# Pairs of neighbouring PSUM banks for score runs, and new rule tables for the order planner of a gated attention + MLP kernel

## The chip, the core and the metric

The kernel runs on one core of one Trainium2 chip. The metric is the device time of one execution in microseconds (us); the time before is 664.01 us, the median of three runs (663.37 to 664.15). A core has a matmul engine (PE), which writes only into PSUM (8 banks of 128 partitions x 512 fp32 here), and three engines that work on tiles: ACT (exponentials), DVE and POOL. SP issues most of the transfers. Each engine takes its instructions strictly from its own list and stops at the first one whose semaphores are not yet up; so the order of each list is decided before the kernel runs.

## What is computed

Two branches over the same 2048 x 512 input are mixed by a gate. In the kernel, everything is bf16 with fp32 sums in PSUM.

```python
x = A_x
g = _sigmoid((x * gate_w).sum(-1, keepdims=True))
# a: 32 heads of 16: qkv = x @ wqkv; scores = q k^T / 4; p = softmax(scores); o = p v; a = o @ wo
# b: (x @ w_gate) * (x @ w_up) @ w_down, inner width 1376
return g * a + (1 - g) * b
```

The scores are 32 heads x 2048 x 2048, and each needs an exponential: this is what ACT, and in part DVE, spend their time on.

## The kernel before, in words

**Tiles on PE.** Almost every matmul uses a 64 x 32 part of the array. The 128 rows are split in two halves (`r` = 0 or 1 in the code), the 128 columns in four. A *batch* is four matmuls of 512 columns on one half, one for each column part (`pe64`; with new weights it shows as L1674, with weights that are still held from the batch before as L1652). Two batches on different halves stream at the same time. One pass of both halves, eight matmuls, is called a *turn* below.

**Three kinds of batches.** *Scores* (`QM,KT`): the keys of 128 positions against 512 queries, one bank for each head of a group of four heads; 2,048 banks in all. *PV* (`Vp` or `Vs` as weights): the exponentiated scores times V, with a column of ones for the denominators. *Fill* (`u`, `g`, `k`, `q`, `v`, `do` units; weights named `xT`, `wu`, `wg`, `wd`, `wk`, `wq`, `wo`): projections, the MLP and the output. A fill unit takes 8 batches in most cases and then a single evacuation of one bank; a score batch takes one evacuation for each batch.

**Two kinds of score steps.** A step is four heads x 128 keys x 512 queries. An *A* step is exponentiated by ACT (`exp`, L1771) from PSUM into cells of `PT` or of buffers that are free at the time (`xT`, `wd`, `wu`, `wg`, `wo`, `hT`); one instruction can take two banks if they are neighbours. It has two PV batches. A *D* step is done on DVE by writing integers whose bits are a bf16 exponential (`dpass`, L1811, into `DB`, `wv`, `wk`); three shifted copies of it are made by POOL (L1818) or DVE (L1817), and PV runs over the four versions with scaled V, eight batches, so that the error averages out. So a D step costs PE six batches more than an A step.

**The planner.** `_Sched` simulates the engines while it writes their lists. Whenever half `r` is free in its model, `pe_phase` (L677) offers it, in a fixed order, the start of an A score (`s_a`, L313), of a D score (`s_d`, L343), a PV batch (`v_job`, L388) or a fill batch (`f_cont`, `f_start`). Some 35 named rules (how many A scores may be outstanding, how far one half may run ahead, how long ACT waits for a neighbour, and so on) are tables over the model's time: `g(name)` (L177) reads the entry for the present slot of 4 us. `bank_pick` (L273) chooses one of the free banks; for A scores it looks for one next to the bank taken last, or one that has a free neighbour, but it takes one bank at a time, and nothing keeps the neighbour for the mate. `try_act` (L741) joins two ready A scores in one instruction where their banks are neighbours. The delays in this model (0.216 us for a batch, 0.05 us from an engine's end to the next engine's start, and so on) are constants in the code. `emit` then turns the dependencies into semaphore waits.

Of the kernel before, what the change touches and what calls it, by code (L numbers as in the profile page):

```python
# [136 lines left out]
class _Sched:  # L137
# [134 lines left out]

    def bank_pick(self, kind, r):  # L273

        fr = self.bfree
        if kind == "A":
# [24 lines left out]
        best = None  # L301
# [10 lines left out]

    def s_a(self, r):  # L313
# [11 lines left out]
        bank = self.bank_get("A")  # L325
# [8 lines left out]
        self.log("pe%d" % r, 0.216, ("SA", e.q, e.kt, ci, bank))  # L334
        self.take(r, 0.216)
# [7 lines left out]
    def s_d(self, r):  # L343
        i = self.dpos[r]
        if not self.bfree or self.nb["D"] >= self.g("dmax"):
            return False
        if len(self.bfree) <= self.g("ares") and self.nb["A"] < self.g("amin"):
            return False
        if i - self.dpos[1 - r] >= self.g("skewd") or (self.g("lw") > 1 and i % 2 == 0 and len(self.bfree) < 2):
            return False  # L350
# [6 lines left out]
        bank = self.bank_get("D", r)  # L357
# [8 lines left out]
        self.log("pe%d" % r, 0.216, ("SD", e.q, e.kt, ci, bank))  # L366
        self.take(r, 0.216)
# [20 lines left out]
    def v_job(self, r):  # L388
# [43 lines left out]
        self.ofree[p] = self.now + 0.385 + 0.05  # L432
        self.at(self.ofree[p])
        self.log("pe%d" % r, 0.216, ("V", e.q, e.kt, e.kind, v))
        self.take(r, 0.216)
        done = self.now + 0.385 + 0.05
# [124 lines left out]
    def f_slice(self, u, r):  # L561
# [15 lines left out]
        self.log("pe%d" % r, u.slot, ("F", u.name, r, i))  # L577
        self.take(r, u.slot)
        if u.pos == u.n:
            end = self.now + 0.385 + max(0.0, u.slot - 0.216)  # L580
            if u.ph == 0:
                u.ph, u.half, u.pos = 1, 1 - r, 0
                u.okt = end + 0.07
# [45 lines left out]
    def f_start(self, r):  # L629
# [4 lines left out]
        if sum(1 for u in self.fact if u.ph == 0) >= self.g("fstart"):  # L634
            return False
# [94 lines left out]

    def evenly(self, l):
# [9 lines left out]
    def try_act(self):  # L741
# [26 lines left out]
        if grp is not None:  # L768
# [3 lines left out]
            if len(fr) > 1:  # L772
                for i in range(len(rd)):
                    j = next((j for j in range(i + 1, len(rd)) if abs(rd[j][4] - rd[i][4]) == 1), None)
                    if j is not None and (i == 0 or self.g("apick")):
# [5 lines left out]
                        if self.g("tri"):  # L781
                            lo, hi = min(x[4], y[4]) - 1, max(x[4], y[4]) + 1
                            z = next((z for z in rd if z[4] == lo or z[4] == hi), None)
# [8 lines left out]
                if n == 1 and any(abs(x[4] - rd[0][4]) == 1 and x[0] <= self.now + self.g("await") for x in self.aready):  # L792
# [10 lines left out]
        dur = 0.42667 * n + 0.0635  # L803
# [10 lines left out]
        t = self.now + dur + 0.11 + 0.05  # L814
# [67 lines left out]
    def dve_pass(self, now):  # L882
        mate, hold = None, False
        if self.dready and self.dready[0][0] <= now and self.g("dpair"):
            x = self.dready[0]
            for y in sorted(self.dready, key=lambda y: y[:2])[1:]:
                if abs(y[4] - x[4]) == 1 and (y[2] is x[2] or max(x[2].buf, y[2].buf) < self.par["ND"]):
# [4 lines left out]
        if self.dready and self.dready[0][0] <= now and (mate or not hold):  # L892
# [17 lines left out]
            self.at(t + 0.05, lambda: [self.bank_put(b, [op]) for b in bks])  # L910
            for y in xs:
# [4 lines left out]
                if e.npass == 4:  # L916
# [5 lines left out]
                    for r in (0, 1):  # L922
                        self.vq[r].append((t + 0.05, e, 0, e.ydone))
                    self.at(t + 0.05)
# [10 lines left out]
    def copy_dve(self):  # L935
        now = self.now + 1e-9
        for e in self.cpq:
# [17 lines left out]
            self.cp_done(e, v, hs, op, self.now + dur + self.DEND + 0.05)  # L955
# [124 lines left out]
    def q_evac(self, c, b):  # L1080
        def f(sc, u, last):
# [3 lines left out]
            sc.at(sc.now + 0.681 + 0.05, lambda: sc.bank_put(bk, [op]))  # L1085
            sc.at(sc.now + 0.681 + 0.05, lambda: (sc.qpend.append((k, op)), sc.q_try()))
# [31 lines left out]
    def o_evac(self, m, vops):  # L1118
# [14 lines left out]
        t = self.now + 0.681 + 0.05  # L1133
# [90 lines left out]
    def norm3(self, bi, o):  # L1224
# [3 lines left out]
        self.setr(("ot", bi), self.now + 0.598 + self.DEND + 0.05, op)  # L1228


    def simple(self, dur, dend, key, make, after=None):


        def f(sc, u, last):
            op = make(u, last) if sc.hw else None
            bk = u.bank
            t = sc.now + dur + dend + 0.05
# [7 lines left out]
    def setup(self):  # L1245
# [29 lines left out]
        def mk_x(ch, t):  # L1275
            def ev(sc, u, last):
# [3 lines left out]
                tq = sc.now + ND + DE + 0.05  # L1280
# [69 lines left out]
        def mk_do(c, tt):  # L1350
            t = 4 * c + tt

            def ev(sc, u, last):
# [9 lines left out]
                tq = sc.now + 0.658 + DE + 0.05  # L1363
# [123 lines left out]
    def run(self):  # L1487
# [17 lines left out]
        self.aout = self.dout = 0  # L1505
        self.aready, self.dready = [], []
# [76 lines left out]
class _Hw:  # L1583
# [179 lines left out]
    def exp(self, banks, cells, deps):  # L1763
        g, i = cells[0]
        t = self.grp[g]
        if len(banks) > 1:
            dst = t[:, i : cells[-1][1] + 1 : cells[1][1] - i, :]
            src = self.ps[:, banks[0] : banks[-1] + 1, :]
# [227 lines left out]
    def prologue(self):  # L1996
# [113 lines left out]
        for var in (0, 1):  # L2110
# [22 lines left out]
 'alook': ((127, 2), (1, 3), (9, 2), (2, 6), (41, 2)),  # L2133
# [3 lines left out]
 'amax': ((1, 4), (2, 3), (1, 6), (2, 5), (1, 4), (2, 5), (21, 4), (6, 5), (24, 4), (2, 5), (6, 7), (1, 6), (20, 4), (1, 7), (1, 4), (1, 6), (1, 5),  # L2137
          (30, 4), (2, 7), (3, 4), (1, 5), (1, 4), (2, 5), (5, 4), (2, 6), (2, 4), (3, 6), (1, 4), (1, 6), (5, 4), (3, 6), (6, 5), (20, 6)),
 'amin': ((7, 4), (5, 3), (8, 1), (16, 3), (2, 1), (11, 0), (1, 1), (2, 3), (4, 0), (1, 3), (3, 0), (2, 2), (6, 3), (1, 1), (5, 2), (5, 0), (2, 1),
          (4, 3), (6, 0), (1, 3), (2, 2), (4, 3), (1, 2), (1, 0), (1, 2), (1, 3), (2, 2), (4, 4), (5, 2), (6, 1), (1, 0), (9, 3), (3, 0), (19, 3),  # L2140
          (8, 2), (1, 3), (20, 2)),
 'apick': ((12, 1), (1, 0), (23, 1), (33, 0), (5, 1), (5, 0), (4, 1), (8, 0), (2, 1), (1, 0), (4, 1), (1, 0), (20, 1), (9, 0), (1, 1), (11, 0),
           (1, 1), (2, 0), (3, 1), (5, 0), (2, 1), (7, 0), (20, 1)),
 'ares': ((3, 2), (9, 1), (1, 3), (1, 2), (6, 1), (1, 3), (4, 2), (7, 3), (4, 2), (10, 3), (4, 0), (1, 2), (5, 1), (4, 2), (2, 1), (6, 0), (1, 1),
          (1, 2), (4, 1), (1, 0), (1, 2), (3, 3), (1, 1), (3, 2), (7, 1), (1, 2), (1, 3), (2, 2), (4, 0), (14, 2), (3, 3), (4, 2), (1, 1), (4, 3),
          (1, 1), (3, 3), (1, 0), (3, 2), (9, 3), (3, 2), (2, 3), (5, 2), (5, 0), (3, 2), (1, 3), (20, 2)),
 'await': ((1, 0.6), (2, 0), (3, 0.2), (1, 0.3), (3, 0.1), (4, 0), (3, 0.1), (19, 0), (17, 0.05), (2, 0), (5, 0.05), (2, 0), (6, 0.05), (1, 0),
           (3, 0.05), (2, 0.1), (5, 0.05), (1, 0.1), (5, 0.05), (2, 0), (4, 0.05), (1, 0.3), (6, 0), (8, 0.1), (2, 0.4), (3, 0.05), (1, 0.1),
           (13, 0.05), (4, 0), (1, 0.1), (2, 0), (9, 0.05), (10, 0), (9, 0.05), (20, 0)),
 'cpmax': ((1, 20), (2, 14), (3, 8), (1, 14), (1, 20), (2, 8), (2, 10), (24, 14), (12, 10), (1, 3), (1, 30), (10, 14), (2, 30), (7, 14), (5, 5),  # L2150
           (5, 10), (1, 20), (1, 10), (2, 8), (2, 10), (2, 8), (4, 30), (6, 5), (1, 20), (2, 5), (1, 10), (11, 5), (3, 8), (2, 20), (2, 30), (1, 8),
           (5, 30), (7, 8), (3, 30), (6, 8), (5, 30), (1, 20), (1, 10), (3, 20), (7, 14), (2, 3), (20, 14)),
 'dact': ((10, 2), (2, 5), (2, 2), (10, 5), (1, 3), (2, 2), (7, 3), (15, 2), (1, 4), (7, 2), (3, 3), (9, 5), (2, 2), (3, 4), (11, 2), (6, 5), (19, 2),
          (7, 5), (15, 2), (3, 4), (2, 5), (2, 3), (2, 5), (6, 2), (1, 5), (6, 2), (26, 3)),
 'dahead': ((3, 0), (3, 1), (2, 2), (2, 0), (1, 2), (1, 0), (1, 1), (11, 2), (1, 1), (4, 2), (7, 0), (5, 2), (2, 1), (10, 2), (7, 1), (8, 2), (1, 1),
            (10, 2), (1, 1), (1, 2), (2, 1), (32, 2), (2, 1), (9, 2), (2, 1), (7, 2), (6, 1), (5, 2), (2, 1), (3, 0), (9, 2), (20, 0)),
 'dend': ((1, 2), (1, 0), (1, 5), (3, 2), (2, 0), (4, 2), (5, 1), (3, 4), (8, 1), (2, 3), (7, 1), (5, 3), (10, 2), (4, 5), (9, 2), (1, 5), (17, 0),
          (4, 2), (3, 0), (1, 2), (6, 3), (1, 2), (2, 3), (1, 5), (1, 3), (8, 0), (5, 3), (7, 0), (3, 2), (7, 1), (3, 2), (2, 1), (4, 3), (2, 0),
          (1, 1), (2, 0), (1, 2), (1, 4), (3, 3), (29, 4)),
# [146 lines left out]
```

## Time and profile before

| | |
|---|---|
| median of three runs | 664.01 us |
| the profiled execution, first to last instruction (its span) | 667.2 us |
| PE | 658.8 us busy, 22,835 matmuls |
| ACT | 647.0 us busy, 995 instructions |
| DVE | 605.0 us busy, 1000 instructions |
| POOL | 548.8 us busy, 640 instructions |
| granted TensorE clock | 0.999 |

The profiled execution's own time is its span, 3.2 us above the median. A busy PE in this table is a PE with at least one matmul in flight: with two halves, one of them may stand still while the engine counts as busy. So the number of matmuls in a stretch of time says more than the busy share. The busy times of ACT and DVE include the end of an instruction that overlaps the next one's start, so that durations in the groups are longer than the distance from start to start.

### The profile page before, as it was taken

To read this page: it belongs to the slowest core of one execution; us is meant where nothing else is said; L and a number is where in the kernel's file an instruction comes from. 1 tells how busy PE (TensorE), PEld (TensorE's weight loads), DVE (VectorE), ACT (ScalarE), POOL (GpSimd) and SP (SyncE) were. 2 spreads that over 40 slices of the span, in tenths; PEclk is the share of its full clock that TensorE was granted. 3 is DMA by queue.
4 is the path that set the end of the run, shared out by engine and by line. 5 is a ranking of instruction groups with operands and counts; after the bars stand their busy time and mean duration, and the time that the engine had idled before them with its cause. 6 is when DMAs were issued, how large, how long until landed. Compare 5 with 4: busy or idle time off the path is not lost.

```text
span 667.2 us, 47435 instructions
## 1 busy us (share of the span) xinstructions
PE 658.8 (99%) x22835; PEld 368.4 (55%) x20907; DVE 605.0 (91%) x1000; ACT 647.0 (97%) x995; POOL 548.8 (82%) x640
## 2 busy tenths in 40 slices
PE   8999999999999999999999999999999999999997
PEld 4565555565555555555555565555555565555553
DVE  6899989999998998999999898999999887898885
ACT  5999999999999999999999999999999999999995
POOL 3576899898999868998998879899998997784781
PEclk9999999999999999999999999999999999999999
DMA  9201211212221100001011010100001010000101
GB/s 177 61 5 30 65 31 50 61 28 55 74 61 26 38 20 26 26 12 30 13 21 29 16 42 21 31 13 17 25 14 28 21 38 23 16 25 15 34 21 36
DMA packets 32120, 22.95 MB, mean 34 GB/s; under 512 B 17356, under 2 KB 28524, under 8 KB 31920
## 3 DMA queue, kind: packets, MB, share of 16 engines
q1 hardware_dynamic: 30784, 18.86, 11.5%
q8 instruction: 171, 2.80, 1.8%
q0 software_dynamic: 176, 0.53, 0.3%
q10 hardware_dynamic: 960, 0.52, 0.3%
q14 instruction: 29, 0.24, 0.1%
HBM read 12.23 MB, written 2.36 MB: 22 GB/s over the span
## 4 chain that ended last, share of the span: by engine, by line
PE 98%; DMA 1%; DVE 1%; issue 0%; ACT 0%; ACTq 0%
PE ps L1674 88%; PE ps L1652 9%; DMA wq<-in_A_wqkv_dram 1%; PE ps L2086 0%; DVE hT L1956 0%; DVE hT L1953 0%; ACT wu L1771 0%; ACTq L2003 0%; DVE wu L1860 0%; PE ps L1758 0%; ACTq L82 0%
## 5 line engine op out<-in xcount | busy, mean ns | idle before, releaser
L1674 PE MATMUL ps<-QM,KT 64*32 64x512 bf16 x6264 | 460.8, 378 | 1.1 <-issue 0.5
L1818 POOL INT64_ADD DB<-DB x403 | 348.2, 880 | 68.1 <-PE ps L1674 24.5
L1811 DVE TENSOR_SCALAR DB<-ps 128x512 int16<-128x512 f32 (+1 forms) x565 | 370.2, 692 | 36.0 <-PE ps L1674 32.2
L1771 ACT ACTIVATE PT<-ps 128x512 bf16<-128x512 f32 (+1 forms) x538 | 372.6, 799 | 2.0 <-PE ps L1674 1.2
L1674 PE MATMUL ps<-DB,Vs 64*17 64x512 bf16 x3536 | 312.3, 376 | 0.0
L1674 PEld LDWEIGHTS ps<-QM,KT 64*32 64x32 bf16 x6264 | 141.5, 90 | 136.4 <-DVE DB L1811 27.6
L1674 PE MATMUL ps<-PT,Vp 64*17 64x512 bf16 x1476 | 211.5, 376 | 0.1
L1771 ACT ACTIVATE xT<-ps 128x512 bf16<-128x512 f32 (+1 forms) x286 | 204.1, 808 | 0.9 <-PE ps L1674 0.4
L1652 PE MATMUL ps<-QM,KT 64*32 64x512 bf16 x1928 | 187.9, 376 | 0.1
L1674 PE MATMUL ps<-xT,Vp 64*17 64x512 bf16 x786 | 140.6, 376 | 0.0
L1674 PE MATMUL ps<-DB,Vp 64*17 64x512 bf16 x1144 | 112.9, 376 | 0.0
L1674 PE MATMUL ps<-xT,wg 64*32 64x512 bf16 x1376 | 110.0, 377 | 0.0
L1674 PE MATMUL ps<-xT,wu 64*32 64x512 bf16 x1376 | 107.3, 376 | 0.0
L1674 PEld LDWEIGHTS ps<-DB,Vs 64*17 64x17 bf16 x3536 | 88.5, 86 | 32.5 <-PE ps L1674 6.6
L1674 PE MATMUL ps<-wd,hT 64*32 64x512 bf16 x1408 | 100.5, 376 | 0.0
L1771 ACT ACTIVATE wd<-ps 128x512 bf16<-128x512 f32 (+1 forms) x93 | 66.3, 795 | 1.1 <-PE ps L1674 1.1
L1674 PEld LDWEIGHTS ps<-PT,Vp 64*17 64x17 bf16 x1476 | 54.0, 86 | 14.6 <-PE ps L1674 2.6
L1818 POOL INT64_ADD wv<-DB x59 | 51.7, 881 | 6.7 <-DVE DB L1811 2.5
L1818 POOL INT64_ADD DB<-wv x58 | 51.2, 899 | 6.6 <-PE ps L1652 2.4
L1818 POOL INT64_ADD DB<-wk x57 | 49.8, 890 | 6.7 <-DVE OT L1977 3.4
L1811 DVE TENSOR_SCALAR wv<-ps 128x512 int16<-128x512 f32 x72 | 47.0, 685 | 1.9 <-PE ps L1674 1.3
L1811 DVE TENSOR_SCALAR wk<-ps 128x512 int16<-128x512 f32 x66 | 43.7, 700 | 2.1 <-PE ps L1674 2.0
(120 smaller groups left out, 858.0 us busy)
## 6 DMA issues: line engine op xcount, KB each, us to landing
rb<-rscr SPq DMA_DIRECT2D x16, 256.0 KB
QM<-qraw SPq DMA_DIRECT2D x124, 16.0 KB, 2.3
oc<-oraw SPq DMA_DIRECT2D x60, 32.0 KB, 2.3
out_dram<-ost SPq DMA_DIRECT2D x12, 128.0 KB, 1.7
wd<-in_B_w_down_dram SPq DMA_DIRECT2D x10, 128.0 KB, 2.1
wu<-in_B_w_up_dram SPq DMA_DIRECT2D x12, 96.0 KB, 2.2
wg<-in_B_w_gate_dram SPq DMA_DIRECT2D x12, 96.0 KB, 2.2
OT<-in_A_x_dram SPq DMA_DIRECT2D x2, 256.0 KB, 4.9
```

What stands on the lines that cost most here:

```text
L1652: return pe.add_instruction(mybir.InstMatmult(name=self.nc.get_next_instruction_name(), engine=pe.engine, ins=[pe.lower_ap(rhs), pe.lower_ ...
L1674: o = pe.matmul(dst, lhs, rhs, start=st, stop=sp, tile_position=(64 * r, 32 * cc), skip_group_check=True)
L1771: return self.P.op("act", lambda a: a.activation(dst, src, ACT.Exp, scale=self.ES), deps)
L1811: return self.dve(lambda v: v.tensor_scalar(dst, src, self.YB, 0.0, ALU.add, ALU.max), deps)
L1818: return self.P.op("pool", lambda e: e.int64_add(o.bitcast(I64), a.bitcast(I64), 32 * v * 0x0001000100010001), deps)
```

## The change

It does three things, all in the planner; the instructions that the engines know, the tiles, the prologue and the tail are as before.

1. **Pairs of banks.** A half that begins the first of the two scores of its step may take two neighbouring free banks at once (`pair_pick`, `take_pair`); the second bank is kept in `apend` or `dpend` for the second score. The rule `apair` says when: 0 never, 1 if there is such a pair, 2 only so; 3 and 4 also take two banks that are not neighbours. `dpair` over 3 does the same for D scores. The second score of such a pair is no longer held back by the limits on outstanding scores and on how far a half may run ahead.
2. **Delays of the model.** A batch takes 0.2168 us in place of 0.216 (`pk`); the time from an evacuation to the next writer of the bank is 0.055 in place of 0.05 for DVE and 0.168 in place of 0.16 for ACT; the change of half in an output bank is 0.075 in place of 0.05.
3. **Tables.** All rules are read in slots of 1 us in place of 4 us and have new entries, most of them three slots long; `flim` (a limit on the started fill work) is new. One line shows the kind; the others are alike.

```diff
+    def take_pair(self, kind, p):
+        for x in p:
+            self.bfree.remove(x)
+            self.nb[kind] += 1
+            self.bkind[x] = kind
+        return p
+
+    def pair_pick(self, far):
+        if self.par["anyb"]:
+            return self.bfree[:2] if len(self.bfree) > 1 else None
+        best = None
+        for b in self.bfree:
+            if b + 1 in self.bfree:
+                x = (b - 1 in self.bfree) + (b + 2 in self.bfree)
+                if best is None or x < best[0]:
+                    best = (x, b)
+        if best is None:
+            return self.bfree[:2] if far and len(self.bfree) > 1 else None
+        return [best[1], best[1] + 1]
...
     def s_a(self, r):
         i = self.apos[r]
-        if not self.bfree or self.nb["A"] >= self.g("amax"):
-            return False
-        if i - self.apos[1 - r] >= self.g("skew") or (self.g("lw") > 1 and i % 2 == 0 and len(self.bfree) < 2):
-            return False
+        p = None
+        if self.apend[r] is None:
+            if not self.bfree or self.nb["A"] >= self.g("amax"):
+                return False
+            if i - self.apos[1 - r] >= self.g("skew") or (self.g("lw") > 1 and i % 2 == 0 and len(self.bfree) < 2):
+                return False
+            if i % 2 == 0 and self.g("apair"):
+                p = self.pair_pick(self.g("apair") > 2) if self.nb["A"] + 2 <= self.g("amax") else None
+                if p is None and self.g("apair") in (2, 4):
+                    return False
...
-        bank = self.bank_get("A")
+        if self.apend[r] is not None:
+            bank, self.apend[r] = self.apend[r], None
+        elif p is not None:
+            bank, self.apend[r] = self.take_pair("A", p)
+        else:
+            bank = self.bank_get("A")
...
-        t = self.now + dur + 0.11 + 0.05
+        t = self.now + dur + 0.168
...
+        if sum((2 - x.ph) * x.n - x.pos for x in self.fact) > self.g("flim"):
+            return False
...
- 'lw': ((72, 1), (2, 0), (45, 1), (1, 0), (5, 1), (3, 0), (4, 1), (7, 2), (41, 1)),
...
+ 'pk': 0.2168,
...
- 'slot': 4.0,
+ 'slot': 1.0,
```

What the planner makes of it is seen in the lists. Of the 2,048 score banks ACT takes 1,336 before and 1,352 now (four steps moved from D to A); it needs 981 instructions for them before, 355 of them with two banks, and 798 now, 554 of them with two banks. PE has 22,837 matmuls in its list before (two of them have no record in the profile) and 22,741 now. POOL has 645 and 612 instructions, DVE 1000 and 1002, SP 368 in both.

The first place is ACT's list at its 268th score bank, 144.8 us into the profiled execution before. Rows with 128x512 take one bank, rows with 128x1024 or 128x2x512 two. Before:

```order
L1771 ACTIVATE wd<-ps 128x512 x5
L1771 ACTIVATE PT<-ps 128x512
L1771 ACTIVATE wd<-ps 128x512 x3
L1771 ACTIVATE PT<-ps 128x512
L1771 ACTIVATE wd<-ps 128x512
L1771 ACTIVATE wd<-ps 128x2x512 x2
L1771 ACTIVATE wd<-ps 128x512
```

and at the same bank now:

```order
L1824 ACTIVATE wd<-ps 128x2x512
L1824 ACTIVATE PT<-ps 128x2x512 x2
L1824 ACTIVATE wd<-ps 128x2x512 x5
L1824 ACTIVATE PT<-ps 128x2x512
L1824 ACTIVATE wd<-ps 128x2x512
```

The single banks have become pairs: 16 banks in 14 instructions before, 20 banks in 10 now.

The second place is PE's list from its 2,600th matmul, some 86 us into the execution before; `xT,wg` and `xT,wq` or `xT,wk` are fill, a name in brackets is the engine whose semaphore the row waits for. Before:

```order
L1674 MATMUL ps<-QM,KT 32x512 [waits s_act]
L1674 MATMUL ps<-QM,KT 32x512 x7
L1674 MATMUL ps<-PT,Vp 17x512
L1674 MATMUL ps<-wd,Vp 17x512
L1674 MATMUL ps<-PT,Vp 17x512
L1674 MATMUL ps<-wd,Vp 17x512
L1674 MATMUL ps<-xT,wg 32x512 x4
L1674 MATMUL ps<-DB,Vs 17x512 [waits s_pool]
L1674 MATMUL ps<-DB,Vs 17x512 x3
L1674 MATMUL ps<-QM,KT 32x512 [waits s_dve]
```

and now:

```order
L1727 MATMUL ps<-QM,KT 32x512 [waits s_act]
L1727 MATMUL ps<-QM,KT 32x512 x3
L1727 MATMUL ps<-xT,wk 32x512 x4
L1705 MATMUL ps<-QM,KT 32x512 x4
L1727 MATMUL ps<-wd,Vp 17x512 [waits s_pe1]
L1727 MATMUL ps<-PT,Vp 17x512
L1727 MATMUL ps<-wd,Vp 17x512
L1727 MATMUL ps<-PT,Vp 17x512
L1727 MATMUL ps<-QM,KT 32x512 [waits s_dve]
```

A score that waits for ACT is now followed by a fill batch on the other half and then by its mate in the second bank of the pair, which waits for nothing and keeps the weights; before, two scores stood back to back. Over the whole list 1,697 of the 2,048 score batches begin with a wait before, and 1,487 now. Of the 3,335 matmuls from the 70th to the 3,404th (the ones that run from 10 to 110 us before), 1,060 are fill before and 1,148 now.

More of the change, by code (lines that the diff above doesn't have):

```diff
@@ L333, in s_a @@
         self.s_count(c, b, r, op)
-        self.log("pe%d" % r, 0.216, ("SA", e.q, e.kt, ci, bank))
-        self.take(r, 0.216)
+        self.log("pe%d" % r, self.par["pk"], ("SA", e.q, e.kt, ci, bank))
+        self.take(r, self.par["pk"])
         t = self.now + 0.385 + 0.056
@@ L344, in s_d @@
         i = self.dpos[r]
[L345 to L350, printed above, removed]
+        p = None
+        if self.dpend[r] is None:
+            if not self.bfree or self.nb["D"] >= self.g("dmax"):
+                return False
+            if len(self.bfree) <= self.g("ares") and self.nb["A"] < self.g("amin"):
+                return False
+            if i - self.dpos[1 - r] >= self.g("skewd") or (self.g("lw") > 1 and i % 2 == 0 and len(self.bfree) < 2):
+                return False
+            if i % 2 == 0 and self.g("dpair") > 3:
+                p = self.pair_pick(self.g("dpair") > 5) if self.nb["D"] + 2 <= self.g("dmax") else None
+                if p is None and self.g("dpair") in (5, 7):
+                    return False
         if i // 2 >= len(self.dsteps) and not self.next_d():
@@ L356, in s_d @@
         self.dpos[r] += 1
-        bank = self.bank_get("D", r)
+        if self.dpend[r] is not None:
+            bank, self.dpend[r] = self.dpend[r], None
+        elif p is not None:
+            bank, self.dpend[r] = self.take_pair("D", p)
+        else:
+            bank = self.bank_get("D", r)
         ci = 2 * r + i % 2
@@ L365, in s_d @@
         self.s_count(c, b, r, op)
-        self.log("pe%d" % r, 0.216, ("SD", e.q, e.kt, ci, bank))
-        self.take(r, 0.216)
+        self.log("pe%d" % r, self.par["pk"], ("SD", e.q, e.kt, ci, bank))
+        self.take(r, self.par["pk"])
         t = self.now + 0.385 + 0.056
@@ L431, in v_job @@
         self.vl[p][r] = op
-        self.ofree[p] = self.now + 0.385 + 0.05
+        self.ofree[p] = self.now + 0.385 + 0.075
         self.at(self.ofree[p])
-        self.log("pe%d" % r, 0.216, ("V", e.q, e.kt, e.kind, v))
-        self.take(r, 0.216)
-        done = self.now + 0.385 + 0.05
+        self.log("pe%d" % r, self.par["pk"], ("V", e.q, e.kt, e.kind, v))
+        self.take(r, self.par["pk"])
+        done = self.now + 0.385 + 0.055
         if e.kind == "A":
@@ L576, in f_slice @@
         self.fdone += 1
-        self.log("pe%d" % r, u.slot, ("F", u.name, r, i))
-        self.take(r, u.slot)
+        self.log("pe%d" % r, self.par["pk"], ("F", u.name, r, i))
+        self.take(r, self.par["pk"])
         if u.pos == u.n:
-            end = self.now + 0.385 + max(0.0, u.slot - 0.216)
+            end = self.now + 0.385
             if u.ph == 0:
                 u.ph, u.half, u.pos = 1, 1 - r, 0
-                u.okt = end + 0.07
+                u.okt = end + 0.075
                 u.first = op
@@ L728, in target, with spaced @@
         return x + (y - x) * (p - a) / (b - a)
+    def spaced(self, x, y, z):
+        a, b, c = sorted((x, y, z))
+        return b - a == c - b and (self.par["anyb"] or b - a == 1)
     def evenly(self, l):
@@ L773, in try_act @@
                 for i in range(len(rd)):
-                    j = next((j for j in range(i + 1, len(rd)) if abs(rd[j][4] - rd[i][4]) == 1), None)
+                    j = next((j for j in range(i + 1, len(rd)) if self.near(rd[j][4], rd[i][4])), None)
                     if j is not None and (i == 0 or self.g("apick")):
@@ L781, in try_act @@
                         if self.g("tri"):
-                            lo, hi = min(x[4], y[4]) - 1, max(x[4], y[4]) + 1
-                            z = next((z for z in rd if z[4] == lo or z[4] == hi), None)
+                            z = next((z for z in rd if self.spaced(x[4], y[4], z[4])), None)
                         if z is not None:
@@ L791, in try_act @@
                         break
-                if n == 1 and any(abs(x[4] - rd[0][4]) == 1 and x[0] <= self.now + self.g("await") for x in self.aready):
+                if n == 1 and any(self.near(x[4], rd[0][4]) and x[0] <= self.now + self.g("await") for x in self.aready):
                     n = 0
@@ L802, in try_act @@
         rd.sort(key=lambda x: x[4])
[L803 removed]
+        dur = 0.42667 * n + self.par["act0"]
         deps = []
@@ L886, in dve_pass @@
             for y in sorted(self.dready, key=lambda y: y[:2])[1:]:
-                if abs(y[4] - x[4]) == 1 and (y[2] is x[2] or max(x[2].buf, y[2].buf) < self.par["ND"]):
+                if self.near(y[4], x[4]) and (y[2] is x[2] or max(x[2].buf, y[2].buf) < self.par["ND"]):
                     if y[0] <= now:
@@ L1132, in o_evac @@
         self.dve_go(0.598, ("O", m))
-        t = self.now + 0.681 + 0.05
+        t = self.now + 0.681 + 0.055
         if m % 8 == 7 and c < 3:
@@ L1236, in f @@
             bk = u.bank
-            t = sc.now + dur + dend + 0.05
+            t = sc.now + dur + dend + 0.055
             sc.at(t, lambda: sc.bank_put(bk, [op]))
```

150 lines of the change are left out of this document (61 added, 89 removed), and 180 rows, old and new, of the table PAR.

## Prediction

> **What bounds the kernel now.** I read the page first, for the span and the engine on the chain of waits.
>
> ```profile
> span 667.2 us, 47435 instructions
> PE 658.8 (99%) x22835; PEld 368.4 (55%) x20907; DVE 605.0 (91%) x1000; ACT 647.0 (97%) x995; POOL 548.8 (82%) x640
> PE 98%; DMA 1%; DVE 1%; issue 0%; ACT 0%; ACTq 0%
> ```
>
> PE is on the chain for 98% of it, but its 99% cannot be taken as "full": PE counts as busy while one of its halves stands still. So I looked in the timeline for a stretch where one half is never short of work, to get the price of a batch.
>
> ```profile
> 302.06 0.39 PE L1674 MATMUL ps<-xT,wg 64*32 64x512 bf16 x4
> 302.28 0.39 PE L1674 MATMUL ps<-xT,wg 64*32 64x512 bf16 x4
> 302.49 0.39 PE L1674 MATMUL ps<-QM,KT 64*32 64x512 bf16 x4
> 302.71 0.39 PE L1652 MATMUL ps<-QM,KT 64*32 64x512 bf16 x4
> 302.92 0.39 PE L1674 MATMUL ps<-xT,wg 64*32 64x512 bf16 x4
> 303.14 0.39 PE L1674 MATMUL ps<-QM,KT 64*32 64x512 bf16 x4
> 303.36 0.39 PE L1674 MATMUL ps<-xT,wg 64*32 64x512 bf16 x4
> ```
>
> Six batches follow each other in 303.36 - 302.06 = 1.30 us: 0.217 us each. With both halves at work that is eight matmuls per 0.217 us. Then the table of stretches of 50 us, for how many matmuls PE really did:
>
> ```profile
> 0.00:10.00 10.00, 8.02 (x69) 1.00 0.88 190
> 10.00:60.00 50.00, 49.17 (x1656) 1.00 0.23 47
> 60.00:110.00 50.00, 49.55 (x1679) 1.00 0.19 49
> 110.00:160.00 50.00, 49.84 (x1740) 1.00 0.21 47
> 210.00:260.00 50.00, 50.00 (x1801) 1.00 0.10 26
> 610.00:660.00 50.00, 49.78 (x1748) 1.00 0.09 24
> 660.00:667.20 7.20, 2.71 (x88) 0.92 0.23 75
> ```
>
> Between 10 and 660 us there are 22,835 - 69 - 88 = 22,678 matmuls. At full rate they need 22,678 / 8 x 0.217 = 615 us of the 650. **So 35 us, some 5%, are lost by one half or the other, and nothing in the change's reach is worth more than that.** The loss is uneven. The first two stretches hold 3,335 matmuls (90.5 us of 100; 9.5 lost), the other eleven 19,343, 1,758 each (525 of 550; 25 lost). Against the average of the others the first two are 181 matmuls short, 181 / 8 x 0.217 = 4.9 us.
>
> What a half waits for when its next batch is late shows best on the weight-load track, since a batch that is held by a semaphore is held at its weight load. From the table of waits of that track:
>
> ```profile
> PEld ps L1674 <- DVE DB L1811: 31.9, 152, 0.4
> PEld ps L1674 <- ACT PT L1771: 23.5, 109, 0.4
> PEld ps L1674 <- issue: 23.3, 88, 0.6
> PEld ps L1674 <- PE ps L1674: 23.0, 95, 0.6
> PEld ps L1674 <- ACT xT L1771: 10.8, 52, 0.3
> ```
>
> These are gaps on the load track, much of them under a matmul that still streams, so they are shares and not losses. Evacuations of score banks by DVE and by ACT are the two large releasers: the next score wants a bank that isn't free yet, and since the list is in order, the other half's next batch stands behind it. ACT itself is nearly full:
>
> ```profile
> L1771 ACT ACTIVATE PT<-ps 128x1024 bf16<-128x1024 f32 x200 | 200.9, 1051 | 1.2 <-PE ps L1674 0.5 <-PE ps L1652 0.2
> L1771 ACT ACTIVATE PT<-ps 128x512 bf16<-128x512 f32 x338 | 188.0, 649 | 0.8 <-PE ps L1674 0.7
> 66.78 2.87 ACT L1771 ACTIVATE PT<-ps 128x1024 bf16<-128x1024 f32 x3
> 620.37 2.55 ACT L1771 ACTIVATE xT<-ps 128x512 bf16<-128x512 f32 x5
> ```
>
> The last two rows give distances from start to start: three pairs in 2.87 us with a last one of 1.05, so (2.87 - 1.05) / 2 = 0.91 us for a pair; five single banks in 2.55, (2.55 - 0.65) / 4 = 0.48 for one. All of ACT's score work of before, 626 singles and 355 pairs, is 300 + 323 = 623 us of the 650. PE's 615 and ACT's 623 are close to each other and to the span: two engines that feed each other, each with 4 to 5% to spare, and the waits between them are what an order can change.
>
> **The change part by part.**
>
> *A. Fewer PV batches.* Four steps move from D to A. Each D step has 24 matmuls more, so 96 matmuls, 12 turns of 0.217 us, leave PE: **-2.6 us**. What pays for them is ACT, below. On DVE and POOL 16 evacuations and twelve copies go; both were covered by PE before.
>
> *B. Fill work earlier.* From the 70th to the 3,404th matmul the list has 88 more fill matmuls and as many fewer scores and PV. Ten of the banks that had to be evacuated in those 100 us are gone, and fill has one evacuation for eight batches. This is the place where 4.9 us are missing against the rest. Bounds: nothing, or all of 4.9. The fill share goes from 32 to 34% there, against 26.5% later with less loss, so the share alone is not what makes the rest better; I take half, **-2.5 us**.
>
> *C. Waits of scores.* 1,697 score batches that begin with a wait become 1,487, 12% fewer. If the loss outside the first 100 us shrank with them, 12% of 25 us is **-3.0 us**. Bounds: nothing, since a wait that is written down is not always a wait that is felt, or a third, -8.3 us, if the corrected delays (0.055 for 0.05, 0.075 for 0.05) remove also those stalls which the planner had not foreseen.
>
> *D. Pairs.* 199 more pairs. On ACT's side, a pair saves 2 x 0.48 - 0.91 = 0.05 us, 10 us in all; 16 more banks cost 16 x 0.48 = 7.7. Net -2.3 us on an engine that isn't on the chain: nothing for the sum, and it is cover if PE gets faster. On PSUM's side a pair is dearer: its first bank is given back only with the second, after 1.05 us in place of 0.65, so 199 x 0.40 = 80 us of one bank, over eight banks 10 us. Bounds: 0 and **+10**. Which end is nearer? One stretch of before has pairs nearly throughout, another has singles:
>
> ```profile
> L1771 ACT ACTIVATE wd<-ps 128x1024 bf16<-128x1024 f32 x30 | 29.2, 1042 | 0.3 <-PE ps L1674 0.3
> L1771 ACT ACTIVATE PT<-ps 128x1024 bf16<-128x1024 f32 x20 | 20.0, 1036 | 0.5 <-PE ps L1674 0.5
> PEld ps L1674 <- ACT PT L1771: 1.2, 6, 0.2
> PEld ps L1674 <- ACT wd L1771: 1.0, 5, 0.3
> ...
> L1771 ACT ACTIVATE PT<-ps 128x512 bf16<-128x512 f32 x37 | 20.8, 665 | 0.0
> L1771 ACT ACTIVATE xT<-ps 128x512 bf16<-128x512 f32 x34 | 19.2, 697 | 0.0
> PEld ps L1674 <- ACT PT L1771: 2.3, 11, 0.3
> PEld ps L1674 <- ACT xT L1771: 1.5, 6, 0.3
> ```
>
> The first four rows are 60 to 110 us, the others 560 to 610. With pairs the load track waited 11 times for ACT (2.2 us), with singles 17 times (3.8 us). So pairs as such do not make PE wait for ACT. I take a tenth of the upper end, **+1.0 us**.
>
> Sum: -2.6 - 2.5 - 3.0 + 1.0 = -7.1; 667.2 - 7.1 = 660.1 us of span. The runs' median was 3.2 us below the profiled one: **656.9 us**, 1.1% faster.
>
> The Trainium skill has a rule that speaks against this sum. "TensorEngine Tiling (Array Packing)", section "PSUM Bottleneck", says that packing the array speeds up TensorE but not the evacuation of PSUM, which may then become the bottleneck. By that rule turns saved on PE are worth nothing and only ACT's relief counts. The trace bears it out in part: ACT is at 623 of 650 us, PE at 615. This is the second rival.
>
> **The rivals.**
>
> 1. *The planner's new order is kept by the hardware throughout.* Then B is all of 4.9, C a third, 8.3, D nothing: 667.2 - 2.6 - 4.9 - 8.3 = 651.4, **648.2 us** as a run. For it: a loss of 35 us leaves room for it. Against it: "issue", 23.3 us on the load track, is not a thing that an order removes.
> 2. *ACT sets the pace.* Then PE's turns are free and ACT's 2.3 us are the gain: 664.9, **661.7 us**. For it: in 560 to 610 us ACT has no idle at all before its rows (0.0 behind both). Against it: PE, not ACT, is on the chain.
> 3. *Slower: pairs run out of banks.* The mechanism is D at its upper end: 10 us of bank time, with B and C lost since a score then waits for two banks: 667.2 - 2.6 + 10 = 674.6, **671.4 us**. It decides as soon as PE asks for a pair while fewer than two neighbours are free, which is more likely where the output tile and fill hold banks. Against it: the rows of 60 to 110 us.
> 4. *The rules change the list but not the time.* The waits that vanish come back at the next score, and what A takes from PE is lost to them: **664 us**. For it: of the waits that go, most are second scores of a pair, whose first score still waits.
>
> **How the numbers follow.** Forecast 0.48; rival 1 0.20; rival 2 0.12; rival 3 0.12; rival 4 0.08. The likeliest gives 656.9. What a measurement of this kernel can tell from no change is about 0.2%, 1.3 us, so faster is below 662.7 and slower above 665.3. Forecast and rival 1 are faster, rival 2 by a margin of 1 us, so I count 0.11 of its 0.12 there: faster 0.79; same 0.08 + 0.01 = 0.09; slower 0.12. The range goes from a little below rival 1 to the edge of rival 4, 646.0 to 665.0, and leaves out rival 3 and what lies below rival 1. The likeliest case by itself, with C between nothing and a third and D between 0 and 3, is 651 to 662.
>
> **What would show it.** In the profile after: PE x22,739 or so (A). The matmuls from 10 to 60 and 60 to 110 us: B is right if they come to 1,700 and more each, and wrong if they stay below 1,690. The later stretches: 1,775 and more on average for C. ACT near 800 instructions, and its waits on the load track not above 34 us in total for PT and xT together (23.5 + 10.8 before); more is D on its way to rival 3. Rival 2 would show as ACT without idle in every stretch while PE's count per stretch stays where it was. The prediction falls with a count per stretch that stays under 1,740 in the later part, for then neither order nor delays were what held PE.

## The result, and the profile after

The changed kernel takes 659.23 us (median of 4 runs, 659.04 to 660.67), the kernel before 663.74 us (4 runs). The ratio is 0.9939, 95% interval 0.9927 to 0.9951: **4.5 us, 0.6% faster**, with 656.9 forecast and 646 to 665 as the range. Sign and range are right; of the 7.1 us forecast, 4.5 came. All ratios in this document leave out one single execution, of s_act below, which took 2,388.6 us where its other eleven took 670.5 to 676.1.

The page of the changed kernel: span, busy times of the engines, instruction queue, shares of the chain of waits.

```profile
span 657.3 us, 46640 instructions
PE 650.2 (99%) x22739; PEld 364.1 (55%) x20515; DVE 606.6 (92%) x1002; ACT 640.3 (97%) x812; POOL 523.1 (80%) x607
...
q8 instruction: 169, 2.77, 1.7%
...
PE 98%; DMA 1%; DVE 0%; issue 0%; ACT 0%; ACTq 0%
```

PE's 22,739 matmuls are those that the list had promised (22,741, of which two again have no record). Its weight loads fell from 20,907 to 20,515, of which the prediction said nothing. The table of stretches of the changed kernel (start:end, length, PE's busy us, its matmuls, granted clock, DMA share, GB/s):

```profile
10.00:60.00 50.00, 49.30 (x1695) 1.00 0.26 51
60.00:110.00 50.00, 50.00 (x1764) 1.00 0.21 55
160.00:210.00 50.00, 50.00 (x1728) 1.00 0.17 48
510.00:560.00 50.00, 49.93 (x1825) 1.00 0.10 27
560.00:610.00 50.00, 50.00 (x1818) 1.00 0.07 18
```

A matmul that lies on a border is counted in both stretches. For the sum I therefore take two long stretches, first of the kernel before and then of the changed one:

```profile
10.00:110.00 100.00, 98.72 (x3319) 1.00 0.21 48
110.00:610.00 500.00, 499.57 (x17652) 1.00 0.11 29
```

```profile
10.00:110.00 100.00, 99.30 (x3448) 1.00 0.24 53
110.00:610.00 500.00, 499.93 (x17774) 1.00 0.11 29
```

The changed kernel does 129 matmuls more from 10 to 110 us (129 / 8 x 0.217 = 3.5 us) and 122 more from 110 to 610 (3.3 us), and has 96 fewer to do (2.6 us). That is 9.4 of the 9.9 us between the two spans.

**But 9.9 is not the change's.** In every run whose span is known, but for those of one kernel (e_nudge below, 2.1 to 2.2), the time is the span plus 1.8 or 1.9 us (659.11 for 657.3). By that the profiled execution of before, 667.2, was one of 669.0 us, while its timed runs were at 663.4 to 664.2. It lay 5.0 us above their median and not 3.2, as was said ahead of the prediction, where the span was taken for the time. So 5 us of the difference between the two profiles belong to that one execution. The weight-load track of the changed kernel shows what differs most (us, times, longest):

```profile
PEld ps L1727 <- DVE DB L1864: 43.0, 195, 0.4
PEld ps L1727 <- ACT PT L1824: 22.1, 108, 0.4
PEld ps L1727 <- PE ps L1727: 21.8, 92, 0.6
PEld ps L1727 <- ACT xT L1824: 14.6, 75, 0.3
PEld ps L1727 <- issue: 6.3, 23, 0.6
```

"issue", PE waiting for nothing that the profile shows, fell from 23.3 to 6.3 us. The waits for ACT on PT and xT are what they were (36.7 against 34.3), those for DVE on DB are longer (43.0 against 31.9).

### The profile page after: what moved, and what is told of

Its sections match the earlier page's. It is cut to its first block, busy times and chain, and to the rows that moved or that the text cites. A ratio compares the mean times of both kernels' runs of the same rounds, so it can differ in the third digit from the quotient of the medians.

```text
span 657.3 us, 46640 instructions
## 1 busy us (share of the span) xinstructions
PE 650.2 (99%) x22739; PEld 364.1 (55%) x20515; DVE 606.6 (92%) x1002; ACT 640.3 (97%) x812; POOL 523.1 (80%) x607
## 3 DMA queue, kind: packets, MB, share of 16 engines
q8 instruction: 169, 2.77, 1.7%
## 4 chain that ended last, share of the span: by engine, by line
PE 98%; DMA 1%; DVE 0%; issue 0%; ACT 0%; ACTq 0%
PE ps L1727 87%; PE ps L1705 10%; DMA wq<-in_A_wqkv_dram 1%; PE ps L2139 0%; DVE hT L2009 0%; DVE hT L2006 0%; ACT wu L1824 0%; ACTq L2056 0%; PE ps L1811 0%; ACTq L82 0%
## 5 line engine op out<-in xcount | busy, mean ns | idle before, releaser
L1727 PE MATMUL ps<-QM,KT 64*32 64x512 bf16 x5968 | 450.4, 378 | 0.3 <-ACT wu L1824 0.3
L1864 DVE TENSOR_SCALAR DB<-ps 128x512 int16<-128x512 f32 x563 | 367.8, 687 | 27.0 <-PE ps L1727 24.0
L1871 POOL INT64_ADD DB<-DB x374 | 330.8, 900 | 75.6 <-DVE DB L1864 19.2
L1824 ACT ACTIVATE PT<-ps 128x1024 bf16<-128x1024 f32 (+1 forms) x368 | 313.5, 950 | 0.5 <-PE ps L1705 0.3
L1727 PE MATMUL ps<-DB,Vs 64*17 64x512 bf16 x3424 | 300.6, 376 | 0.1
L1824 ACT ACTIVATE xT<-ps 128x1024 bf16<-128x1024 f32 (+1 forms) x271 | 240.8, 965 | 0.2
L1705 PE MATMUL ps<-QM,KT 64*32 64x512 bf16 x2224 | 215.9, 376 | 0.0
L1727 PE MATMUL ps<-PT,Vp 64*17 64x512 bf16 x1274 | 176.7, 376 | 0.0
L1727 PE MATMUL ps<-xT,Vp 64*17 64x512 bf16 x974 | 144.8, 376 | 0.0
L1824 ACT ACTIVATE wd<-ps 128x1024 bf16<-128x1024 f32 (+1 forms) x83 | 67.8, 936 | 0.0
L1864 DVE TENSOR_SCALAR wv<-ps 128x512 int16<-128x512 f32 (+1 forms) x70 | 47.3, 701 | 2.9 <-PE ps L1727 2.1
L1727 PEld LDWEIGHTS ps<-PT,Vp 64*17 64x17 bf16 x1274 | 43.8, 86 | 10.7 <-PE ps L1727 1.4
L1871 POOL INT64_ADD wk<-DB x46 | 41.7, 910 | 8.4 <-PE ps L1727 2.3
```

What stands on the lines that cost most here:

```text
L1705: return pe.add_instruction(mybir.InstMatmult(name=self.nc.get_next_instruction_name(), engine=pe.engine, ins=[pe.lower_ap(rhs), pe.lower_ ...
L1727: o = pe.matmul(dst, lhs, rhs, start=st, stop=sp, tile_position=(64 * r, 32 * cc), skip_group_check=True)
L1824: return self.P.op("act", lambda a: a.activation(dst, src, ACT.Exp, scale=self.ES), deps)
L1864: return self.dve(lambda v: v.tensor_scalar(dst, src, self.YB, 0.0, ALU.add, ALU.max), deps)
L1871: return self.P.op("pool", lambda e: e.int64_add(o.bitcast(I64), a.bitcast(I64), 32 * v * 0x0001000100010001), deps)
```

## The experiments

Three theories: **PE** (PE's list, walked in order by both halves, sets the end: turns saved or held up count), **ACT** (rival 2 of the prediction), and **fit** (the rules are worth what the one list that they were searched for is worth; neither the pair rule nor the delays have a value by themselves). The kernels ran on three chips, and the same kernel before took 669.67, 666.27 and 664.13 us on them; only ratios to before on the same chip are compared. The changed kernel stands at 0.9939, and 0.9931 when run again on one of the three; that it stands there on the other two as well is assumed. Ratios of two kernels on different chips carry both intervals, some 0.3% together (2 us). Each ratio is given with its interval; the quotient of two medians can differ from it within that (1.0076 in place of 1.0059 for the first kernel with added work).

### The two kernels again

> The kernel before, unchanged, for a second profile. The profile of before on which the prediction's terms rest has a span of 667.2 us, 3.2 us above its timed runs; the profile after has 657.3 us, 1.8 us below its own. If the first was an ordinary execution, this one has again some 667 us and some 23 us of 'issue' gaps on the weight-load track. If the first profile held stalls that the timed runs do not have, this one has 661 to 663 us and fewer such gaps; then the loss of 35 us that the prediction worked with was really about 30, and its terms B and C were sized too large by the same share.

Before: 669.03 us, 0.9986 (0.9960 to 1.0011), on a chip where before takes 669.67. Its stretches and its "issue":

```profile
10.00:110.00 100.00, 99.00 (x3321) 1.00 0.22 48
110.00:610.00 500.00, 499.10 (x17596) 1.00 0.11 29
...
PEld ps L1674 <- issue: 24.2, 86, 0.8
```

It agrees with the first profile of before in the span (668.7) and in "issue". So the prediction was made on an execution of the kind that this chip shows, and its runs were of another kind. Which chip that first profile came from is not known.

> The changed kernel unchanged, as the base for the runs with added work, timed in the same way beside the kernel before. If the result holds on any chip: 0.994 of before, with a profile that has 5 to 15 us of 'issue' gaps on the weight-load track against the 23 to 24 us of the two profiles of before. If part of the gain came from one profile or one chip: 0.997 or more.

After, on the second chip: 661.42 us against 666.27, 0.9931 (0.9908 to 0.9954). The gain is the same on a chip on which both are slower.

```profile
10.00:110.00 100.00, 99.52 (x3439) 1.00 0.23 52
110.00:610.00 500.00, 499.44 (x17661) 1.00 0.11 28
...
PEld ps L1727 <- issue: 11.4, 39, 0.6
```

The first stretch repeats (3,439 and 3,448 after; 3,319 and 3,321 before). The second does not: 17,661 here, 17,774 in the first profile, and 17,652 and 17,596 before. What was read there as a gain is as large as what one kernel differs by between two executions.

### What a microsecond of work on each engine costs

The list of the changed kernel is kept and one engine is given extra work.

PE: the first batch of every `u` unit is done twice (44 batches, up to 9.5 us).

```diff
+        if kind == "u" and start:
+            self.pe64(r, mms, deps)
+            deps = []
         return self.pe64(r, mms, deps)
```

> The changed kernel with one batch done twice in each of the 44 u units (the first one, which overwrites, so nothing else changes): 44 more batches on PE, everything else in the same order. Each leaves the other half idle or fills a slot that was idle anyway: 44 x 0.217 = 9.5 us at most; by the list, with each half one batch at a time, 32 x 0.217 = 6.9 us. If PE's list sets the pace (prediction): slower by 5.5 to 9.5 us, some 665 to 669. If ACT sets the pace (rival 2): slower by less than 2 us.

674.75 us, 1.0059 (1.0036 to 1.0082): 1.2% over the changed kernel, some 8 us for at most 9.5 us of PE. A turn that is added is paid nearly in full. Not all of it need be the turn itself: the batches also bring 172 weight loads, and "issue" is above that of the two next kernels on this chip (10.7 and 15.0).

```profile
PEld ps L1727 <- issue: 16.9, 52, 1.0
```

ACT: 199 of the 554 double evacuations (5 of 14) are made as two single ones; both banks are given back after the second, as before.

```diff
+        if len(banks) > 1:
+            self.npair = getattr(self, "npair", 0) + 1
+            if self.npair % 14 < 5:
+                o = []
+                for x, y in zip(banks, cells):
+                    o.append(self.P.op("act", lambda a, x=x, y=y: a.activation(t[:, y[1], :], self.ps[:, x, :], ACT.Exp, scale=self.ES), deps))
+                return o[-1]
```

> The changed kernel with 199 of its 554 two-bank instructions on ACT done as two one-bank instructions, in the same place of ACT's list; both banks and cells are still reported only after the second. ACT gets 199 x (2 x 0.48 - 0.91) = 10 us more work, that is, the relief that the pairs gave is taken back; nothing else moves. If PE's list sets the pace: slower by 0 to 3 us, since ACT has about 4% to spare. If ACT sets the pace: slower by 8 to 12 us, some 667 to 671.

671.48 us, 1.0021 (1.0000 to 1.0042): 0.9% over the changed kernel, some 6 us for about 10 us of ACT, between what the two theories had said (0 to 3 and 8 to 12).

The same, but each bank is given back after its own evacuation:

```diff
-            e.eops.append(op)
+            e.eops.append(op[rd.index(x)] if isinstance(op, list) else op)
...
-        bl = [x[4] for x in rd]
-        self.at(t, lambda: [self.bank_put(b, [op]) for b in bl])
+        ops = op if isinstance(op, list) else [op] * n
+        bl = [(x[4], o) for x, o in zip(rd, ops)]
+        self.at(t, lambda: [self.bank_put(b, [o]) for b, o in bl])
```

> As s_act, but each of the two instructions reports its own bank: the first bank of the 199 pairs is free 0.4 us earlier than in s_act. The difference to s_act is the price of holding two banks, term D of the prediction. By the sum (a tenth of 10 us): 1 us faster than s_act or less. If pairs run out of banks (rival 3): 5 to 10 us faster than s_act, and then faster than the changed kernel itself unless ACT sets the pace.

670.77 us, 1.0015 (0.9997 to 1.0033). The two differ by 0.7 us in the median and not by their intervals: that a pair holds its first bank until the second is done costs nothing that can be measured. Rival 3, which priced the same 199 pairs at 10 us, is out.

DVE: one `u` copy in three is done twice (16 x 0.685 us, 11 us).

```diff
+        if f % 3 == 0:
+            deps = [self.dve(cp, deps)]
+        return self.dve(cp, deps)
```

> The changed kernel with 16 of the 44 copies of u out of PSUM on DVE done twice, the second after the first has ended: 16 x 0.6 to 0.7 = 10 us more work on DVE, spread over the whole program, nothing else moved. If PE's list sets the pace and evacuations by DVE are its largest releaser (43 us of the load track's gaps after, against 37 for ACT's PT and xT): slower by 2 to 6 us, as each delays the score banks behind it. If DVE has room (92% busy): below 2 us.

672.51 us, 1.0095 (1.0070 to 1.0121): 1.6% over the changed kernel, about 11 us for 11 us of DVE, more than had been expected either way (2 to 6 us, or below 2). The chain of waits and the load track show the same work arriving at PE:

```profile
PE 89%; DVE 10%; issue 1%; ACT 0%; ACTq 0%
...
PEld ps L1727 <- DVE usb L1902: 12.7, 23, 0.9
```

So work added on PE or DVE costs about its own length, on ACT six tenths, each to within some 2 us. The engine that is on the chain for 98% is not the only one at the limit.

### Work taken from DVE

The other direction: all table copies that DVE makes (37) are made by POOL instead, at the same places of the list.

```diff
-        if eng == "dve":
-            return self.dve(lambda e: e.tensor_scalar(o, a, 32.0 * v, None, ALU.add), deps)
```

> The changed kernel's order kept in every row, but the 37 table copies that VectorE makes (28 of 2,048 elements and 9 of 1,024 or so) are made by GpSimd at the same places: VectorE loses some 22 us of work, GpSimd gains some 33 us (523 to about 556 of 657 us). Theory VectorE sets the pace at a price near 1 both ways (11 us of added work cost 11 us): 8 to 20 us faster than the changed kernel, ratio to before 0.963 to 0.982. Theory that the price is paid by added work alone, since the list on TensorE is fitted to the old durations: 0 to 3 us faster, 0.989 to 0.994. Rival: GpSimd, which takes 0.9 us for a copy where VectorE took 0.72, hands the table out later and score differences wait on it: 2 to 10 us slower than the changed kernel, 0.997 to 1.009, with waits of the weight loads on GpSimd rising from under 3 us.

662.62 us, 0.9978 (0.9963 to 0.9993): 0.4% over the changed kernel. Its busy times, chain and the waits of the load track for POOL:

```profile
PE 652.3 (99%) x22739; PEld 364.6 (55%) x20515; DVE 591.8 (90%) x965; ACT 641.1 (97%) x812; POOL 560.3 (85%) x644
...
PE 95%; POOL 2%; DVE 2%; issue 0%; ACT 0%; POOLq 0%; ACTq 0%
...
PEld ps L1727 <- POOL DB L1869: 2.2, 9, 0.3
PEld ps L1727 <- POOL wk L1869: 1.0, 3, 0.5
PEld ps L1727 <- POOL wv L1869: 0.8, 1, 0.8
```

DVE lost 14.8 us of work and PE gained nothing from it. But POOL got 37.2 us more (560.3 against 523.1): the waits for POOL, 1.9 us in the changed kernel, became 4.0, and POOL is now on the chain. The time lies in the band of the rival that POOL hands its copies out later (0.997 to 1.009). A price measured by adding work is thus no promise for moving it elsewhere. That saved work would bring nothing by itself, since it arrives early at a place where the list has nothing to do with it, is argued and not shown: no run takes work from DVE without giving it to another engine. This attempt at a faster version fails.

### Fewer held weights

A batch with the weights of the one before it loads none. Here the 556 held batches load theirs again, 2,224 loads more on PE.

```diff
-                if same:
+                if False:
```

> The changed kernel with the 556 score batches that keep the weights of the batch before (L1705) loading them again: 2,224 more LDWEIGHTS of 0.09 us on a track that is 55% busy, no more matmuls, the same order. If loads hide under the other half's matmuls and nothing else is limited: no change within 1 us. If PE's instruction fetch is close to its limit (171 blocks of 256 instructions in 653 us, one each 3.8 us; a block's load lands about 2.1 us after it is asked for): 2,224 / 256 = 8.7 more blocks, 8.7 x 3.5 to 3.8 = 30 to 33 us slower if it is the limit all the time, 5 to 15 us if only in places; 'issue' gaps on the load track go from 6 to over 40 us.

685.11 us, 1.0296 (1.0259 to 1.0334): 3.7% over the changed kernel, 24 us, between the expectations for a supply of instructions that is short all the time (30 to 33) and one that is short in places (5 to 15).

```profile
PE 669.6 (97%) x22739; PEld 375.7 (54%) x22739; DVE 611.1 (89%) x1002; ACT 651.7 (94%) x812; POOL 523.6 (76%) x607
...
q8 instruction: 178, 2.92, 1.8%
...
PE 96%; issue 2%; DMA 1%; ACT 1%; DVE 0%; ACTq 0%
...
PEld ps L1727 <- issue: 45.9, 95, 2.0
```

The load track is still at 54%; what grew is "issue", from 11.4 us on the same chip to 45.9, with single gaps of 2 us. (This profile is of the longest of the six executions, 691.9 us, so its 45.9 does not belong to the median.) What these gaps wait for can be read from the trace, which has a record for each packet of the instruction queue, q8: all 95 end 1.2 to 1.7 us after such a packet has landed. The packets land 3.8 us apart, so that chance would put one gap in eight there. So what PE waits for in them is its own instructions.

The changed kernel holds 74 batches more than the one before (556 against 482) and so has 296 loads fewer. At 24 us for 2,224 that would be 3 us; that the cost is in proportion is not shown.

### The rules without their list

Four kernels in which the planner writes another list. The changed kernel with the time of a batch in the model at 0.2167 in place of 0.2168:

```diff
- 'pk': 0.2168,
+ 'pk': 0.2167,
```

> The changed kernel with one constant of the planner's clock moved by a ten-thousandth: a batch takes 0.2167 us in place of 0.2168; rules, tables and all other delays as in the change. The planner makes another list of the same kind: 5,650 batches, 481 pairs on ACT, 42 batches less than the change's list. If the gain comes from the pair rule and from better delays, which are all still there: within 2 us of the changed kernel. If it comes from tables that were fitted to one list: the list loses its fit; batches on one half follow each other more often (by the list alone, with one batch at a time on each half, PE needs 3,055 slots of 0.217 us in place of 2,903): 25 to 40 us slower than the change, some 685 to 700 where before has 664.

718.09 us, 1.0781 (1.0757 to 1.0805): 57 us slower than the changed kernel, with the pair rule, the tables and all but 0.0001 of the delays kept.

The kernel before with the same kind of step, 0.2161 for 0.216:

```diff
-        self.take(r, 0.216)
+        self.take(r, 0.2161)
```

> The kernel before with its own rule tables, and one delay of its order model (the time of a matmul batch) changed from 0.216 to 0.2161 us, which makes the planner write another order by the same rules. By the lists: 3,035 batch slots where before has 2,922. Theory fit (a table set is worth something only for the one list it was searched with): slower than before by 113 slots x 0.2163 us = 24 us or more, as the same nudge of the changed kernel, +152 slots, cost 57 us: ratio to before 1.035 to 1.07. Theory rules (tables and delays carry the time in themselves): within 0.5% of before, 0.995 to 1.005. Theory ScalarE (its work sets the pace): 669 single and 346 double evacuations at 0.48 and 0.91 us against 628 and 355 are +11.5 us, ratio 1.017.

705.38 us, 1.0613 (1.0596 to 1.0630).

The old tables with the corrected delays and without the pair rule:

```diff
-        t = self.now + dur + 0.11 + 0.05
+        t = self.now + dur + 0.168
...
+PAR = {'act0': 0.0635, 'anyb': 0, 'apair': 0, 'flim': 99, 'pk': 0.2168,
```

> The kernel before with its old tables and the change's corrected delays alone, pair rule off. By the list: 3,057 batch slots (before 2,922), 771 single and 294 double evacuations. Theory fit: 135 slots x 0.2163 us = 29 us at least, up to 51 us by the factor that the nudged change showed: ratio to before 1.04 to 1.08. Rival (the corrected delays bring the gain by themselves): 0.99 to 1.00. Theory ScalarE: its work rises by 14 us, ratio 1.02.

716.31 us, 1.0782 (1.0766 to 1.0799).

The changed kernel without the pair rule:

```diff
- 'apair': ((41, 0), (6, 1), (3, 0), (3, 1), (27, 0), (9, 1), (3, 0), (15, 2), ...
+ 'apair': 0,
```

with every `dpair` over 3 set to 3.

> The changed kernel with its new tables and delays, the pair rule switched off everywhere (score runs take one bank each as before). By the list: 3,021 batch slots (after 2,903), 527 single and 427 double evacuations (after 246 and 554), 298 held batches (after 556). It has to be read beside the nudged change (ratio 1.078), which keeps the rule and is as little fitted. Theory fit, pair rule worth little: as the nudged one less 34 slots (7 us), plus ScalarE's 19.5 us x 0.6 = 12 us: ratio 1.07 to 1.10. Theory that the pair rule carries the gain: well above the nudged one, 1.10 or more. Theory that the pair rule costs bank time: below the nudged one, 1.03 to 1.06. Theory ScalarE alone: 0.993 + 19.5 us / 664 = 1.022.

712.78 us, 1.0726 (1.0706 to 1.0746).

All four are 6 to 8% slower than the kernel before, whichever part they keep. The waits of the load track in the last of them (in the first, e_nudge, the longest is that for PE itself, 44.3 us):

```profile
PEld ps L1727 <- DVE DB L1864: 42.3, 176, 0.7
PEld ps L1727 <- ACT PT L1824: 32.8, 142, 0.6
PEld ps L1727 <- PE ps L1727: 28.4, 102, 0.6
PEld ps L1727 <- ACT xT L1824: 24.9, 102, 0.9
PEld ps L1727 <- issue: 17.8, 67, 0.9
```

Waits for ACT on PT and xT are up by 21 us (57.7 against 36.7), but ACT isn't fuller: it is busy for 673.4 us, 33 more than in the changed kernel, but for 95% of the longer span. Theory ACT priced the last three lists by their evacuations at 1.017 to 1.022, and they are at 1.06 to 1.08; it falls as the sole cause. The rival that the delays bring the gain by themselves falls too. Theory fit is what is left of the three. The longer lists explain only a part of it: 113 to 152 batch slots more, at 0.217 us, are 24 to 33 of the 41 to 57 us; the rest is time in which PE waits within them.

The pair rule: without it the unfitted list is 0.5% faster than the unfitted list with it. Two unfitted lists of the old rules without it, 1.0613 and 1.0782, differ by 1.7%, so 0.5% between two such lists says nothing. Whether a search without the pair rule would have found as good a list was not tried.

## Why the prediction was right, and where it was not

**The sum.** It gave a span of 660.1; the profile after has 657.3. Then 3.2 us were taken off to come to the timed runs, where 1.8 should have been added to come from a span to its time. The two errors, +2.8 and -5.0, leave the 2.3 us by which 656.9 was too low; that they nearly cancel is luck. The range, 646 to 665, held all cases but rival 3, so that a time within it says little. **The step that failed is "the runs' median was 3.2 us below the profiled one"**: it moved the level and left the terms as they were, although an execution that is 5 us longer has 5 us of loss that the change need not find. The 35 us of loss, of which B and C took their shares, were some 30 in the runs that count. And the sum has no term for the number of PE's instructions (see rival 1).

**A, right in count.** 22,739 matmuls. That twelve turns are worth 2.6 us is supported by the price of a turn added, not shown: no run took turns away alone, and the one run that took work off an engine, by moving copies to POOL, gained nothing.

**B, right.** 129 matmuls more from 10 to 110 us, 3.5 us, between the 2.5 that I took and the upper bound of 4.9; 118 more in the second pair of profiles. The 10 to 60 mark stood at 1,695, between "right" and "wrong"; 60 to 110 passed by far.

**C, mis-sized: nothing can be shown of its 3.0 us.** Between the first two profiles it looks like 3.3, but the changed kernel's second profile has 9 matmuls more than before's first. And the whole gain, 4.5, is less than A and B together (2.6 + 3.5 = 6.1), unless part of B belongs to that one execution of before as well; that can't be told apart without a profile of before at 664 us. The mark for C, 1,775 on average in the later stretches, had no force: rows of 50 us count what lies on a border twice, the prediction's average of 1,758 was formed from a total without these, and by the rows themselves the kernel before had 1,775 already. Waits that are written down, 12% fewer, were not waits that were felt: the load track's waits for evacuations by DVE and ACT became more, not fewer.

**D, right in its size, and its mark wrong.** The 199 more pairs cost nothing measurable in bank time. ACT's waits for PT and xT together passed the mark (36.7, mark 34) and yet the kernel is faster: a gap on the load track is no loss as long as a matmul streams over it. ACT's relief of 2.3 us was counted as nothing; by the price of added work it could be worth 1.4, which no run shows.

**Rival 1** said that "issue" isn't removed by an order. On the chip where before shows 24.2 us of it, the two kernels with split pairs, whose PE list is that of the changed kernel, show these rows (late release first):

```profile
PEld ps L1727 <- issue: 10.7, 35, 0.8
```

```profile
PEld ps L1728 <- issue: 15.0, 56, 0.6
```

So part of it does go with the list. By the same reading of the trace as above, 14.7 of the 23.3 us in the first profile of before (48 of 88 gaps) end 1.1 to 1.7 us after an instruction packet has landed, and 4.2 of 6.3 us (13 of 23 gaps) in the changed kernel; in the second profiles they are 16.3 and 9.5 us. Chance would put one gap in six there. The changed list has 488 PE instructions fewer (96 matmuls and 392 loads), two packets of 171:

```profile
q8 instruction: 171, 2.80, 1.8%
```

Two packets at 3.8 us would be 7.6 us, an estimate and an upper end, against a gain of 4.5. So a shorter instruction list is a rival to A, B and C as the source of the gain. No run separates them. **Rival 2** (ACT sets the pace, 661.7) lies 2.5 us from the result, as near as the forecast, but its reason isn't borne out: PE's and DVE's added work cost more than ACT's. **Rival 4**, the same time, is outside the interval.

What no rival had: that a rule table seems to be worth its list and little more. With one delay moved by 0.0001 us, the same rules gave a list that was 6% slower (the kernel before) and 9% slower (the changed one), and by that the change is the step from one fitted list to another, 0.6%. How the 0.6% divides over fewer turns, more early fill and fewer PE instructions stays open.

## What to carry to other kernels

Before a sum is made, check that the profiled execution is one of the timed ones: compare its span, plus the constant between span and time, with the runs, and take an excess out of the loss, not out of the answer. Where a planner's order is tuned to one list, a part of its rules can't be tested by switching it off, since any switch writes a new list that costs more than the part is worth; freeze the list and change the work. And a price found by adding work to such a list need not hold for work that is taken away or moved.

## What the runs showed of the hardware

PE's instruction supply is near its limit in this kernel. It is delivered in blocks: 169 packets, 2.77 MB, so 16 KB each; 2.77 MB over PE's 22,739 + 20,515 instructions is 64 bytes for one, 256 in a block. The span gives 657.3 / 169 = 3.9 us to a block, and 690.0 / 178 = 3.9 us in the kernel with no held weights: more instructions made the kernel longer at the same pace. In that kernel there are 54 pairs of neighbouring blocks of which PE waited for both; the second landed 3.8 us after the first in the median (3.35 to 4.34). So with nothing but the supply in the way, PE gets a block each 3.8 us, and the changed kernel uses one each 3.8 us on average (3.79 from landing to landing) without waiting for most of them. The four lists of the last experiments use one each 4.0 to 4.2 us, so the supply is not what holds them up. Why a block takes that long is open.

The Trainium skill, "Runtime: NRT & Kernel Launch", section "Instruction fetch mechanics", says that instructions stream in 16 KiB blocks of 256 and that the cost of crossing a block border is "mostly hidden". The size of the block agrees with 2.77 MB in 169 packets; that it is hidden fits the changed kernel (4.2 us in 13 gaps), and not the one with 2,224 more loads (45.9 us in 95 gaps, 24 us of time).

The same program differs by chip: before took 664.13, 666.27 and 669.67 us on three, each run at a granted clock of 0.998 or more. The ratio of the changed kernel to it was 0.993 on the second of these, and 0.994 in the first measurement, where before took 663.74.
